# Spreading the weights' maxima by a product with an identity, and ten filler products per unit of the first batch

## The chip, the cores and the metric

The kernel runs on one core of one Trainium2 chip. The metric is the device time of one execution in microseconds (us); of several runs the median is given.

## The reference

Attention with queries pooled in pairs, followed by a feed-forward layer whose gate is h*cos(h):

```python
q_pool = q.reshape(B, H, S // 2, 2, D).mean(axis=3)          # 8, 8, 1152 -> 576, 64
scores = np.matmul(q_pool, k.transpose(0, 1, 3, 2)) / np.sqrt(D)
scores = scores - np.max(scores, axis=-1, keepdims=True)
attn = np.exp(scores)
attn = attn / (np.sum(attn, axis=-1, keepdims=True) + 1e-09)
x = np.matmul(attn, v)            # then (B*S/2, H*D) = (4608, 512)
h = x @ w_in                      # w_in: 512 x 2048
out = (h * np.cos(h)) @ w_out     # w_out: 2048 x 512
```

q, k and v are f32; the two weights are f64 and are read as pairs of 32-bit words.

## The kernel before

Attention runs over 32 pairs of heads (8 batches of 4 pairs). A pair is ten units: unit 0 takes the 64 rows of each head that fill no tile of 128, units 1 to 9 one block of 128 keys each. A unit has score products on TensorE into the PSUM tile st (one buffer of two banks, lines 851 and 871), exp on ScalarE, and, one unit later, the products with v into the PSUM tiles ava and avb, one for each head of the pair (`av`, lines 919 to 1000). In the first four pairs, which are the first batch (`p < NDIR`), the products with v take f32 operands, four a head and unit, and the trace shows two records for each; from the fifth pair on ScalarE and GpSimd (or VectorE) split exp into two f16 parts, and all products are f16. Beside the units run side jobs for later pairs: loads and transposes of q and k, a first pass of score products into the PSUM tile mx (line 646 and on) whose row maxima VectorE takes (mxs, line 656), and the maximum over all of v, which `all_max_begin` spreads over the partitions by way of DRAM (row, am).

The weights are prepared meanwhile. `weight_group` loads slices of 1 MB (wraw), takes each partition's maximum (wmx, line 437), puts the f64 words together as f32 (lines 444 to 450), and needs the maximum over all partitions for a power-of-two scale. To get it, it writes the column of maxima to DRAM (row, line 468), reads it back broadcast to all partitions (wam, line 470), gives the generator four idle steps (WBN), and reduces on VectorE (line 477) with some small operations behind (lines 479 to 490). ScalarE scales and casts, and GpSimd subtracts for the low part (lines 496 to 498). `weight_steps` (line 506) drives these groups: first w_in, two slices a group and two groups alive, then w_out, two slices a group and one group alive. The loop over the units steps it SRATE times a unit.

The feed-forward part (`ffn1`, line 1149, and `ffn2`, line 1205) works on chunks of 256 rows of x, interleaved with later pairs, from when the first batch's x is there, and ends the kernel alone.

What each engine runs in what order is written by `arrange`: it takes the recorded instructions with their dependences, lets a planner with a price for each instruction run them (the lowest place in the recorded order first among those that are ready), and fixes each engine's order by that. The DMAs all go through SP's queue, in order. The waits between engines come from the tiles that are written and read.

Of the kernel before, what the change touches and what calls it, by code (L numbers as in the profile page):

```python
# [19 lines left out]
P = 128  # L20
POW2_MASK = 0x7F800000
POW2_HIGH = 0x40000000
TINY = 1e-12
PMAX = 2.0**6
MDIV = 64.0
VLAG = 3
# [10 lines left out]
DFIRST = 0  # L37
WPOOL = 1
NDIR = 4
WLD = 2  # L40
WBN = 4
WGATE = 4
SRATE = 1.6
EWR = 2

_INS = ["q", "k", "v", "moe_w_in", "moe_w_out"]
# [8 lines left out]
SIZES = {"float32": 4, "uint32": 4, "int32": 4, "float16": 2}  # L55
SEM = 0.10
BOOST = {}


def boxes(ins):  # L60
# [63 lines left out]
    return wr[0][2] if wr else 1  # L124


def arrange(tc, nc, extra):

    rec = [i for i in nc.cur_bb.bb.instructions if "Boundary" not in type(i).__name__]
    nodes, last_pe = [], None  # L130
    for i in rec:
        rd, wr = boxes(i)
        eng = str(i.engine).split(".")[-1]
        if eng == "PE":
            key = wr[0][0].name
            if last_pe is not None and last_pe["key"] == key and len(last_pe["ins"]) < 12:
                nd = last_pe
            else:
                nd = last_pe = dict(eng=eng, ins=[], rd=[], wr=[], cost=0.0, lock=False, key=key)
                nd["tile"] = None  # L140
                nodes.append(nd)
            size = tuple(i.tile_size)
            c = max(n_out(wr) * 0.000421, 0.027)
            if rd[0][4] == 4:
                c = 0.3
            if size[0] == 64 and tuple(i.tile_position)[0] == 64:
                c = 0.0
            nd["cost"] += c
            nd["tile"] = size[0]
        else:  # L150
            nd = dict(eng=eng, ins=[], rd=[], wr=[], cost=0.0, lock=False)
            nodes.append(nd)
            if eng == "SP":
                nd["cost"] = 0.06
                nd["dma"], nd["lat"] = transfer(type(i).__name__, rd[0], wr[0])
            else:
# [10 lines left out]
    for k, nd in enumerate(nodes):  # L167
        deps = set()
        for w, lst in ((0, nd["rd"]), (1, nd["wr"])):
            for t, box, *_ in lst:  # L170
                name = t.name
                if name not in hist:
                    hist[name] = ([], [], set())
                    tag = getattr(t, "tag", None)
                    if tag:
                        base, pool = tag.rsplit("_", 2)[0:2]
                        nb = BUFS.get(base, POOL_BUFS.get(pool, 1))
                        ring = tags.setdefault(tag, [])
                        if pool != "fix" and len(ring) >= nb:
                            prev_tile[name] = ring[-nb]  # L180
                        if pool != "fix" and ring:
                            deps.add(first[ring[-1]])
                        ring.append(name)
                        first[name] = k
                reads, writes, users = hist[name]
                if name in prev_tile:
                    deps |= hist[prev_tile[name]][2]
                deps |= {j for j, bx in writes if hit(bx, box)}
                if str(t.space).endswith("PSUM"):
                    bank = (0, P, box[2] // 2048 * 2048, (box[3] - 1) // 2048 * 2048 + 2048)  # L190
                    deps |= {
                        j
                        for j, bx in reads
                        if hit(bx, bank)
                    }
                if w:
                    deps |= {j for j, bx in reads if hit(bx, box)}
        for w, lst in ((0, nd["rd"]), (1, nd["wr"])):
            for t, box, *_ in lst:
                reads, writes, users = hist[t.name]  # L200
                users.add(k)
                if w:
                    inside = lambda b: box[0] <= b[0] and b[1] <= box[1] and box[2] <= b[2] and b[3] <= box[3]
                    writes[:] = [x for x in writes if not inside(x[1])]
                    reads[:] = [x for x in reads if not inside(x[1])]
                    writes.append((k, box))
                else:
                    reads.append((k, box))
        deps.discard(k)
        nd["deps"] = deps  # L210
# [14 lines left out]
    for k, nd in enumerate(nodes):  # L225
        base = [t.tag.rsplit("_", 2)[0] for t, *_ in nd["rd"] + nd["wr"] if getattr(t, "tag", None)]
        off = 0
        for t in set(base):
            off = min(off, BOOST.get((nd["eng"], t), 0))
        nd["key"] = (k + off, k)  # L230

    engines = ("PE", "Activation", "DVE", "Pool", "SP")
# [79 lines left out]
def tile_attention_ffn(  # L312
# [91 lines left out]
    w1v = w_in.rearrange("(c p) f -> p c f", p=P)  # L404
    w2v = w_out.rearrange("(f p) e -> p f e", p=P)

    w1_ready = [False]
    gate = [None]
    hsc_live = [0]

    def weight_group(wi, i0, fts):
# [6 lines left out]
        for a, ft in enumerate(fts):  # L418
# [45 lines left out]
                    apply_absolute_value=True,  # L464
                )
            yield
        row = dram.tile([n, P], F32, tag="wrow", bufs=4, name="row")
        nc.sync.dma_start(row.rearrange("a p -> p a"), mx)
        am = sb2.tile([P, n, P], F32, tag="g", bufs=NG, name="wam")
        nc.sync.dma_start(  # L470
            am.rearrange("p a b -> p (a b)"),
            row.rearrange("a p -> (a p)").unsqueeze(0).broadcast_to([P, n * P]),
        )
        for _ in range(WBN):
            yield
        mw = sb2.tile([P, n], F32, tag="wmw", name="wmw")
        nc.vector.reduce_max(mw, am, axis=AX.X)
        if wide:
            nc.vector.tensor_scalar_max(mw, mw, 2.0**-15)
            mu = mw.bitcast(U32)  # L480
            ah = sb2.tile([P, n], U32, tag="wah", name="wah")
            nc.vector.tensor_scalar(ah, mu, POW2_HIGH, None, ALU.bitwise_and)
            nc.vector.tensor_scalar(
                mu, mu, 0x07FFFFFF, 3, ALU.bitwise_and, ALU.logical_shift_left
            )
            nc.vector.tensor_tensor(mu, mu, ah, ALU.bitwise_or)
        all_max_end(p2w[:, wi, i0 : i0 + n], mw)
        sc = sb2.tile([P, n], F32, tag="wsc", name="wsc")
        nc.vector.reciprocal(sc, p2w[:, wi, i0 : i0 + n])
        nc.vector.tensor_scalar_mul(sc, sc, 2.0**14)  # L490
        for a, ft in enumerate(fts):
            ds = slice((i0 + a) * width, (i0 + a + 1) * width)
# [13 lines left out]
    def weight_steps():  # L506
        stage = w2[1].rearrange("p f e -> p (f e)").bitcast(F32)
        live = []
        todo = [(wi, i) for wi in range(2) for i in range(0, NWP, 2)]
        done = 0  # L510
        while todo or live:
            if todo and len(live) < (2 if todo[0][0] == 0 else 1):
                wi, i = todo.pop(0)
                if wi == 0:
                    o = i % 4 * 1024
                    fts = [stage[:, o + a * 1024 : o + (a + 1) * 1024] for a in range(2)]
                else:
                    yt = sb1.tile([P, 2, 1024], F32, tag="y", name="wf")
                    fts = [yt[:, a] for a in range(2)]
                live.append(weight_group(wi, i, fts))  # L520
            for g in list(live):
                if next(g, 1) == 1:
                    live.remove(g)
                    done += 2
                    if done == NWP:
# [9 lines left out]
    extra = []  # L535

    def after(ins, prev):
        if prev is not None:
# [369 lines left out]
        return pps  # L908

    acc = [None, None]  # L910
    order = [None]
    xps = {}
    pairs_done = [0]
# [12 lines left out]
    def av(u, parts):  # L926
# [42 lines left out]
        j = i - 1  # L969
        pp = parts[0]  # L970
        if j == 0:
            acc[1] = psum.tile([P, 512], F32, tag="avb", name="avb")[
                :, 0 : QT * (D + 1)
            ].rearrange("p (t d) -> p t d", d=D + 1)
        if p < NDIR:
            for h in range(2):
                first = None
                for t in range(QT):
# [3 lines left out]
                    if start:  # L982
                        first = mm
                    elif first is not None:
                        after(mm, first)
        for part in range(2 if p >= NDIR else 0):
            for h in range(2):
                first = None
# [18 lines left out]
        for h in range(2):  # L1007
            n = QT + 1 - h
            rs = sb2.tile([P, QT + 1], F32, tag="rs", name="rs")
            nc.vector.tensor_scalar_add(rs[:, 0:n], acc[h][:, :, D], 1e-9 * PMAX)  # L1010
# [361 lines left out]
        if pump() is None:  # L1372
            break
    ev_flush()
    arrange(tc, nc, extra)


# [24 lines left out]
```

## Time and profile before

| what | us |
|---|---|
| median of three runs | 1702.73 |
| lowest and highest | 1696.87, 1713.77 |
| the profiled execution | 1703.86 |
| its span, first to last instruction | 1702.1 |
| TensorE busy in it | 1548.4 (91%) |
| VectorE busy | 1134.9 (67%) |
| ScalarE busy | 1216.5 (71%) |
| GpSimd busy | 887.0 (52%) |
| mean granted clock of TensorE | 0.953 |

In the profile PE is TensorE, PEld its weight loads, DVE VectorE, ACT ScalarE, POOL GpSimd, SP SyncE with the DMA queue. The granted clock is a share of 2.4 GHz: 1.00 is that level and 0.50 the level of 1.2 GHz; a value between is a mean over time at both. L851 is line 851 of the kernel. Times in a trace row are from the start of the span.

### The profile page before, as it was taken

The page shows a single profiled execution, that of the slowest core. Times are in us where ns is not written, and L with a number is a line of the kernel's source. Part 1 is how long each engine was busy: PE and PEld are TensorE (multiplying, and loading weights), DVE is VectorE, ACT ScalarE, POOL GpSimd, SP SyncE. Part 2 cuts the span into 40 slices and gives each one's busy share as a digit, 9 for nine tenths or more (in the row PEclk, how much of TensorE's full clock was granted, in tenths as well). Part 3 has the DMA queues.
Part 4 walks back from the last instruction along what each step waited for, and adds up shares of the span by engine and source line. Part 5 has one row for each costly group of instructions (what it writes and reads, how often), then busy time and mean ns, then how long its engine had stood idle before and what let it go on. Part 6 is the DMA issues. An engine that isn't in the chain of part 4 may idle for free.

```text
span 1702.1 us, 39816 instructions
## 1 busy us (share of the span) xinstructions
PE 1548.4 (91%) x16728; PEld 999.9 (59%) x16728; DVE 1134.9 (67%) x1618; ACT 1216.5 (71%) x1476; POOL 887.0 (52%) x763
## 2 busy tenths in 40 slices
PE   2688877899899989998999999899999999997998
PEld 0465655566566546654666566666666666665664
DVE  6667668777776667676877767577777768632342
ACT  2244447888798868876887787798798879884442
POOL 3133227647647565756665556466756575461222
PEclk9687779899999999999999999999999999998999
DMA  9968875233643554354624324434444442101000
GB/s 203 185 117 138 161 142 94 66 69 81 101 79 73 98 99 85 79 105 78 111 59 99 84 52 105 78 72 97 101 78 87 88 112 47 34 21 27 13 25 20
DMA packets 339893, 147.34 MB, mean 87 GB/s; under 512 B 246016, under 2 KB 322816, under 8 KB 339712
## 3 DMA queue, kind: packets, MB, share of 16 engines
q1 hardware_dynamic: 339712, 144.79, 42.9%
q8 instruction: 131, 2.15, 0.6%
q14 instruction: 50, 0.41, 0.1%
HBM read 77.59 MB, written 10.51 MB: 52 GB/s over the span
## 4 chain that ended last, share of the span: by engine, by line
PE 70%; DVE 9%; DMA 8%; ACT 5%; issue 3%; POOL 2%; SPq 1%; another core or an unknown queue 0%; POOLq 0%; ACTq 0%; DVEq 0%
PE f L1205 21%; PE f L1149 19%; PE st L851 12%; PE ava L919 7%; PE avb L919 5%; PE mx L646 4%; DVE mxs L656 2%; DMA qld<-in_q_dram 2%; ACT e L897 2%; DMA am<-row 1%; POOL pp L906 1%; DMA wam<-row 1%; PE mx L686 1%; PE st L871 1%; DMA wraw<-in_moe_w_out_dram 1%
## 5 line engine op out<-in xcount | busy, mean ns | idle before, releaser
L906 POOL TENSOR_TENSOR pp<-e,pp 128x512 f16<-128x512 f32 x374 | 448.3, 1220 | 312.1 <-ACT pp L900 131.5
L1149 PE MATMUL f<-xT,w 128*128 128x256 f16 x3456 | 415.2, 277 | 15.7 <-DVE y L1175 8.9
L897 ACT ACTIVATE e<-st,eb 128x1024 f32<-128x1024 f32 x280 | 311.4, 1112 | 134.4 <-PE st L851 102.8
L656 DVE TENSOR_REDUCE mxs<-mx 128x2 f32<-128x1024 f32 x252 | 307.6, 1221 | 149.6 <-PE mx L646 147.9
L1205 PE MATMUL f<-w,g 128*128 128x512 f16 x1728 | 395.5, 380 | 0.0
L1149 PEld LDWEIGHTS <-w 128*128 128x128 f16 x3456 | 332.0, 99 | 88.0 <-issue 40.2
L900 ACT CAST pp<-e 128x1024 f16<-128x1024 f32 x280 | 292.5, 1044 | 8.9 <-PE ava L919 0.9
L919 PEld LDWEIGHTS <-pp 128*128 128x128 f16 (+1 forms) x7392 | 242.8, 101 | 71.0 <-issue 21.0
L1205 PEld LDWEIGHTS <-g 128*128 128x128 f16 x1728 | 161.2, 98 | 194.4 <-issue 14.5
L1114 POOL TENSOR_TENSOR g<-hsc,g 128x512 f16<-128x512 f32 x144 | 192.2, 1361 | 152.7 <-ACT g L1113 143.2
L919 PE MATMUL ava<-vc,pp 128*128 128x64 f16 (+4 forms) x4784 | 259.0, 205 | 13.2 <-POOL pp L906 10.9
L851 PE MATMUL st<-q1T,k 128*128 128x512 f16 x576 | 228.8, 397 | 14.1 <-ACT e L897 10.0
L851 PE MATMUL st<-q2T,k 128*128 128x512 f16 x576 | 229.1, 398 | 0.0
L919 PE MATMUL avb<-vc,pp 128*128 128x65 f16 (+1 forms) x3312 | 215.4, 205 | 2.6 <-POOL pp L906 2.6
L1175 DVE SCALAR_TENSOR_TENSOR y<-f,r1a,y 128x512 f32<-128x512 f32 x144 | 106.8, 746 | 115.1 <-ACT y L1174 113.6
L851 PEld LDWEIGHTS <-k 128*128 128x128 f16 x1152 | 103.7, 102 | 107.1 <-issue 34.1
L1171 ACT ACTIVATE hsc<-f,r 128x512 f32<-128x512 f32 x144 | 98.3, 684 | 80.5 <-PE f L1149 80.0
L1104 DVE TENSOR_TENSOR hsc<-hsc,y 128x512 f32<-128x512 f32 x144 | 128.5, 942 | 40.3 <-ACT y L1098 39.9
L579 POOL TENSOR_TENSOR kst<-kld,kst 128x512 f16<-128x512 f32 x64 | 88.9, 1390 | 127.0 <-ACT kst L578 119.9
L646 PE MATMUL mx<-k,q1T 64*128 64x512 f16 x504 | 105.8, 415 | 54.0 <-DVE mxs L656 25.8
L902 DVE TENSOR_TENSOR pp<-e,pp 128x1024 f16<-128x1024 f32 x93 | 127.6, 1372 | 37.9 <-ACT pp L900 37.5
L646 PEld LDWEIGHTS <-q1T 64*128 64x128 f16 x512 | 26.8, 94 | 163.1 <-issue 125.9
(113 smaller groups left out, 1561.8 us busy)
## 6 DMA issues: line engine op xcount, KB each, us to landing
vld<-in_v_dram SPq DMA_DIRECT2D x32, 576.0 KB
qld<-in_q_dram SPq DMA_DIRECT2D x64, 256.0 KB
kld<-in_k_dram SPq DMA_DIRECT2D x32, 320.0 KB
kld<-in_k_dram SPq DMA_DIRECT2D x32, 256.0 KB
wraw<-in_moe_w_in_dram SPq DMA_DIRECT2D x8, 1024.0 KB
wraw<-in_moe_w_out_dram SPq DMA_DIRECT2D x8, 1024.0 KB
out_dram<-ob SPq DMA_DIRECT2D x32, 256.0 KB
k<-k SPq DMA_DIRECT2D x64, 80.0 KB
```

Of the source, the lines that this page charges most:

```text
L646: nc.tensor.matmul(m[:, h, :], q1T[n][HALF[h], 2 * t + h, :], k1[n % 3][HALF[h], c * RB : (c + 1) * RB, h, :], start=True, stop=True, skip ...
L656: nc.vector.reduce_max(mxs[n][:, 2 * t : 2 * t + 2, c], m, axis=AX.X)
L851: nc.tensor.matmul(s[:, h, :].rearrange("p (t c) -> p t c", c=P), w[:, j, h, :], x[:, h : 2 * QT : 2, :], start=part == 0, stop=part == 1, ...
L897: nc.scalar.activation(e, s, AF.Exp, scale=exp_scale, bias=eb)
L900: nc.scalar.copy(pp[:, 0], e)
L902: nc.vector.tensor_sub(pp[:, 1], e, pp[:, 0])
L906: nc.gpsimd.tensor_sub(pp[:, 1, c], e[:, c], pp[:, 0, c])
L919: mm = nc.tensor.matmul(out, w, x, start=start, stop=False, skip_group_check=True)
L1104: nc.vector.tensor_mul(hj, hj, y[:, j : j + 2])
L1114: nc.gpsimd.tensor_sub(gt[:, 1], hj, gt[:, 0])
L1149: mm = nc.tensor.matmul(ps[:, fi, :], w1[wt][:, hp, fs], ck.xT[hp][:, xi, cs], start=n == 0, stop=n == 3 * HP - 1, skip_group_check=True,)
L1205: nc.tensor.matmul(po, gt[:, gi, f % 2, ts_], w2[wt][:, f, :], start=f == 0 and (gi, wt) == (0, 0), stop=f == NF - 1 and (gi, wt) == (1, 0),)
```

## The change

The column of maxima is no longer sent through DRAM. An f32 product on TensorE takes it, broadcast along the free dimension, as the stationary operand and an identity as the moving one, into a PSUM tile of the feed-forward part's tag; VectorE reduces from there. The identity is made on GpSimd at the start. The four idle steps of a group go, two of its small operations on VectorE too, SRATE becomes 1.0, and w_out is prepared in groups of one slice, two alive.

In units 1 to 8 of each pair of the first batch, ten f16 products of the identity's bytes with 252 of its columns follow the products with v. They write to columns of avb's bank that nobody reads. The planner sees each as a node of its own at its place in the recorded order, prices an f32 product at 0.112 instead of 0.3, and puts writes to one bank in order.

```diff
-SRATE = 1.6
+SRATE = 1.0
+NFILL = 10
@@ arrange
-            key = wr[0][0].name
+            key = wr[0][0].name if i.name not in fill else i.name
             if rd[0][4] == 4:
-                c = 0.3
+                c = 0.112
                     bank = (0, P, box[2] // 2048 * 2048, (box[3] - 1) // 2048 * 2048 + 2048)
+                    deps |= {j for j, bx in reads if hit(bx, bank)}
+                    if w:
+                        deps |= {j for j, bx in writes if hit(bx, bank)}
@@ tile_attention_ffn
+    ident = sb2.tile([P, P], F32, tag="g", bufs=NG, name="ident")
+    nc.gpsimd.memset(ident, 0.0)
+    nc.gpsimd.affine_select(out=ident, in_=ident, compare_op=ALU.not_equal, fill=1.0,
...
@@ weight_group
-        row = dram.tile([n, P], F32, tag="wrow", bufs=4, name="row")
-        nc.sync.dma_start(row.rearrange("a p -> p a"), mx)
-        am = sb2.tile([P, n, P], F32, tag="g", bufs=NG, name="wam")
-        nc.sync.dma_start(
-            am.rearrange("p a b -> p (a b)"),
-            row.rearrange("a p -> (a p)").unsqueeze(0).broadcast_to([P, n * P]),
-        )
-        for _ in range(WBN):
-            yield
+        am = psum.tile([P, n, P], F32, tag="f", bufs=2, name="wam")
+        for a in range(n):
+            nc.tensor.matmul(
+                am[:, a, :],
+                mx[:, a : a + 1].broadcast_to([P, P]),
+                ident,
...
         mw = sb2.tile([P, n], F32, tag="wmw", name="wmw")
         nc.vector.reduce_max(mw, am, axis=AX.X)
+        pw = p2w[:, wi, i0 : i0 + n]
         if wide:
-            nc.vector.tensor_scalar_max(mw, mw, 2.0**-15)
+            nc.vector.tensor_scalar_max(mw, mw, W64_MIN)
...
-                mu, mu, 0x07FFFFFF, 3, ALU.bitwise_and, ALU.logical_shift_left
-            )
-            nc.vector.tensor_tensor(mu, mu, ah, ALU.bitwise_or)
-        all_max_end(p2w[:, wi, i0 : i0 + n], mw)
+                mu, mu, 0x07F00000, 3, ALU.bitwise_and, ALU.logical_shift_left
+            )
+            nc.vector.tensor_tensor(pw.bitcast(U32), mu, ah, ALU.bitwise_or)
@@ weight_steps
-        todo = [(wi, i) for wi in range(2) for i in range(0, NWP, 2)]
+        todo = [(0, i) for i in range(0, NWP, 2)] + [(1, i) for i in range(NWP)]
-            if todo and len(live) < (2 if todo[0][0] == 0 else 1):
+            if todo and len(live) < 2:
...
-                    fts = [yt[:, a] for a in range(2)]
+                    fts = [yt[:, i % 2]]
@@ av, behind the f32 products with v of one unit
+            i16 = ident.bitcast(F16)
+            for _ in range(NFILL if i < NU - 1 else 0):
+                fm = nc.tensor.matmul(
+                    rest[0],
+                    i16[:, 0:P],
+                    i16[:, 0 : 512 - QT * (D + 1)],
+                    start=False,
+                    stop=False,
+                    skip_group_check=True,
+                )
+                after(fm, mm)
+                fill.add(fm.ins.name)
+                fills.append(fm)
...
+            while h and fills:
+                after(ra, fills.pop())
```

`rest[0]` is the part of avb's bank behind the 260 columns of the products with v.

## Rows read from the trace of the kernel before

**Rows 1.** Part 2 of the page: TensorE's busy tenths and granted clock, forty slices.

```profile
PE   2688877899899989998999999899999999997998
...
PEclk9687779899999999999999999999999999998999
```

**Rows 2.** Windows: us; busy (x instructions) PE, PEld, DVE, ACT, POOL; PEclk, DMA, GB/s.

```profile
36.80:97.75 60.95, 44.47 (x260) 29.30 (x259) 40.43 (x52) 20.44 (x22) 16.15 (x13) 0.72 0.80 165
97.75:147.50 49.75, 40.51 (x274) 29.96 (x273) 36.39 (x60) 22.06 (x24) 11.20 (x6) 0.76 0.81 138
147.50:202.30 54.80, 42.77 (x294) 30.31 (x294) 37.23 (x67) 24.80 (x30) 19.02 (x15) 0.78 0.76 138
202.30:251.75 49.45, 38.53 (x285) 27.38 (x284) 35.62 (x61) 20.58 (x24) 10.73 (x9) 0.83 0.82 159
251.75:274.70 22.95, 18.65 (x265) 12.52 (x265) 20.11 (x27) 18.67 (x23) 19.15 (x15) 0.99 0.77 99
274.70:345.00 70.30, 58.07 (x673) 41.02 (x673) 52.76 (x73) 56.23 (x66) 41.61 (x36) 0.88 0.30 74
```

**Rows 3.** Waits of VectorE, 36 to 275 us: total us, times, longest.

```profile
DVE wmw L477 <- DMA wam<-row: 11.4, 3, 6.3
DVE amx L397 <- DMA am<-row: 10.4, 2, 6.5
DVE wmx L437 <- DMA wraw<-in_moe_w_out_dram: 7.1, 1, 7.1
...
DVE wmx L437 <- DMA wraw<-in_moe_w_in_dram: 3.0, 1, 3.0
```

**Rows 4.** Waits of TensorE, the same stretch and columns.

```profile
PE mx L646 <- DVE mxs L656: 21.4, 7, 5.4
```

**Rows 5.** The chain that ended last, in order of time: start, us, what.

```profile
92.59 8.69 DMA wam<-row
...
119.96 9.72 DMA row<-wmx
...
181.43 1.90 PE ava L919 x8
183.32 1.71 PE avb L919 x8
185.03 1.71 PE st L851 x4
...
196.30 0.89 PE ava L919 x8
197.20 0.86 PE st L851 x4
```

**Rows 6.** Windows of 5 us, columns as in rows 2.

```profile
175.00:180.00 5.00, 0.00 (x0) 0.00 (x0) 0.65 (x1) 0.00 (x0) 0.00 (x0) 0.86 1.25 168
...
190.00:195.00 5.00, 5.00 (x20) 3.17 (x20) 0.12 (x1) 2.51 (x4) 4.80 (x5) 0.50 0.43 52
195.00:200.00 5.00, 5.00 (x34) 3.76 (x35) 4.93 (x6) 1.93 (x4) 1.13 (x1) 0.93 0.75 219
```

**Rows 7.** Waits of SP's queue, 0 to 300 us.

```profile
SPq L470 <- DMA row<-wmx: 12.5, 3, 5.5
```

**Rows 8.** Groups by line on VectorE, 36.8 to 251.8 us: one small operation.

```profile
L401 DVE TENSOR_SCALAR wmw<-wmw 128x2 f32<-128x2 f32 x7 | 1.2, 169 | 0.2
```

**Rows 9.** Timeline of GpSimd at the start; in brackets the idle time before.

```profile
0.73 1.06 POOL L358 MEMSET qs<- 128x1152 f16 x1 [0.29 <-POOLq L1383]
...
9.60 1.40 POOL L585 TENSOR_TENSOR qld<-qld 128x576 f32<-128x576 f32 x1 [4.16 <-DMA qld<-in_q_dram]
```

**Rows 10.** Timeline of TensorE in the feed-forward part.

```profile
313.16 5.40 PE L1149 MATMUL f<-xT,w 128*128 128x256 f16 x48
```

**Rows 11.** Windows of the instructions on slices of weights (wraw): DVE busy, PEclk, DMA, GB/s.

```profile
251.75:274.70 22.95, 5.54 (x5) 0.99 0.77 99
274.70:345.00 70.30, 3.67 (x3) 0.88 0.30 74
```

More of the change, by code (lines that the diff above doesn't have):

```diff
@@ L23 @@
 TINY = 1e-12
+W64_MIN = 0.05859375
 PMAX = 2.0**6
@@ L57 @@
 BOOST = {}
+FILL_LATE = 0
+COLD = 0
 def boxes(ins):
@@ L124, in n_out, with arrange @@
     return wr[0][2] if wr else 1
-def arrange(tc, nc, extra):
+def arrange(tc, nc, extra, fill):
     rec = [i for i in nc.cur_bb.bb.instructions if "Boundary" not in type(i).__name__]
@@ L143, in arrange @@
             c = max(n_out(wr) * 0.000421, 0.027)
+            if COLD and i.name in fill:
+                c = 0.112
             if rd[0][4] == 4:
-                c = 0.3
+                c = 0.112
             if size[0] == 64 and tuple(i.tile_position)[0] == 64:
@@ L190, in arrange @@
                     bank = (0, P, box[2] // 2048 * 2048, (box[3] - 1) // 2048 * 2048 + 2048)
[L191 to L195, printed above, removed]
+                    deps |= {j for j, bx in reads if hit(bx, bank)}
+                    if w:
+                        deps |= {j for j, bx in writes if hit(bx, bank)}
                 if w:
@@ L229, in arrange @@
             off = min(off, BOOST.get((nd["eng"], t), 0))
+        if nd["ins"][0].name in fill:
+            off = FILL_LATE
         nd["key"] = (k + off, k)
@@ L405, in tile_attention_ffn @@
     w2v = w_out.rearrange("(f p) e -> p f e", p=P)
+    ident = sb2.tile([P, P], F32, tag="g", bufs=NG, name="ident")
+    nc.gpsimd.memset(ident, 0.0)
+    nc.gpsimd.affine_select(
+        out=ident,
+        in_=ident,
+        compare_op=ALU.not_equal,
+        fill=1.0,
+        base=0,
+        pattern=[[-1, P]],
+        channel_multiplier=1,
+    )
     w1_ready = [False]
@@ L466, in weight_group @@
             yield
-        row = dram.tile([n, P], F32, tag="wrow", bufs=4, name="row")
-        nc.sync.dma_start(row.rearrange("a p -> p a"), mx)
-        am = sb2.tile([P, n, P], F32, tag="g", bufs=NG, name="wam")
-        nc.sync.dma_start(
-            am.rearrange("p a b -> p (a b)"),
-            row.rearrange("a p -> (a p)").unsqueeze(0).broadcast_to([P, n * P]),
-        )
-        for _ in range(WBN):
-            yield
+        am = psum.tile([P, n, P], F32, tag="f", bufs=2, name="wam")
[4 more added lines that the diff above has]
+                ident,
+                start=True,
+                stop=True,
+                skip_group_check=True,
+            )
         mw = sb2.tile([P, n], F32, tag="wmw", name="wmw")
         nc.vector.reduce_max(mw, am, axis=AX.X)
+        pw = p2w[:, wi, i0 : i0 + n]
         if wide:
-            nc.vector.tensor_scalar_max(mw, mw, 2.0**-15)
+            nc.vector.tensor_scalar_max(mw, mw, W64_MIN)
             mu = mw.bitcast(U32)
@@ L483, in weight_group @@
             nc.vector.tensor_scalar(
-                mu, mu, 0x07FFFFFF, 3, ALU.bitwise_and, ALU.logical_shift_left
+                mu, mu, 0x07F00000, 3, ALU.bitwise_and, ALU.logical_shift_left
             )
-            nc.vector.tensor_tensor(mu, mu, ah, ALU.bitwise_or)
-        all_max_end(p2w[:, wi, i0 : i0 + n], mw)
+            nc.vector.tensor_tensor(pw.bitcast(U32), mu, ah, ALU.bitwise_or)
+        else:
+            all_max_end(pw, mw)
         sc = sb2.tile([P, n], F32, tag="wsc", name="wsc")
-        nc.vector.reciprocal(sc, p2w[:, wi, i0 : i0 + n])
+        nc.vector.reciprocal(sc, pw)
         nc.vector.tensor_scalar_mul(sc, sc, 2.0**14)
@@ L508, in weight_steps @@
         live = []
-        todo = [(wi, i) for wi in range(2) for i in range(0, NWP, 2)]
+        todo = [(0, i) for i in range(0, NWP, 2)] + [(1, i) for i in range(NWP)]
         done = 0
+        yt = None
         while todo or live:
-            if todo and len(live) < (2 if todo[0][0] == 0 else 1):
+            if todo and len(live) < 2:
                 wi, i = todo.pop(0)
@@ L517, in weight_steps @@
                 else:
-                    yt = sb1.tile([P, 2, 1024], F32, tag="y", name="wf")
-                    fts = [yt[:, a] for a in range(2)]
+                    if yt is None:
+                        yt = sb1.tile([P, 2, 1024], F32, tag="y", name="wf")
+                    fts = [yt[:, i % 2]]
                 live.append(weight_group(wi, i, fts))
@@ L523, in weight_steps @@
                     live.remove(g)
-                    done += 2
-                    if done == NWP:
+                    done += 1
+                    if done == NWP // 2:
                         w1_ready[0] = True
@@ L535, in tile_attention_ffn @@
     extra = []
+    fill = set()
     def after(ins, prev):
@@ L910, in tile_attention_ffn @@
     acc = [None, None]
+    rest = [None]
+    fills = []
     order = [None]
@@ L971, in av @@
         if j == 0:
-            acc[1] = psum.tile([P, 512], F32, tag="avb", name="avb")[
-                :, 0 : QT * (D + 1)
-            ].rearrange("p (t d) -> p t d", d=D + 1)
+            bank = psum.tile([P, 512], F32, tag="avb", name="avb")
+            acc[1] = bank[:, 0 : QT * (D + 1)].rearrange("p (t d) -> p t d", d=D + 1)
+            rest[0] = bank[:, QT * (D + 1) :]
         if p < NDIR:
@@ L985, in av @@
                         after(mm, first)
+            i16 = ident.bitcast(F16)
[6 more added lines that the diff above has]
+                    stop=False,
+                    skip_group_check=True,
+                )
+                after(fm, mm)
+                fill.add(fm.ins.name)
+                fills.append(fm)
         for part in range(2 if p >= NDIR else 0):
@@ L1009, in av @@
             rs = sb2.tile([P, QT + 1], F32, tag="rs", name="rs")
-            nc.vector.tensor_scalar_add(rs[:, 0:n], acc[h][:, :, D], 1e-9 * PMAX)
+            ra = nc.vector.tensor_scalar_add(rs[:, 0:n], acc[h][:, :, D], 1e-9 * PMAX)
+            while h and fills:
+                after(ra, fills.pop())
             nc.vector.reciprocal(rs[:, 0:n], rs[:, 0:n])
@@ L1374, in tile_attention_ffn @@
     ev_flush()
-    arrange(tc, nc, extra)
+    arrange(tc, nc, extra, fill)
 def kernel(**inputs):
```

## The prediction

> **What bounds the kernel now.** I read the page's forty slices first [rows 1]. From the ninth slice on TensorE is busy nine tenths or more almost everywhere at a granted clock of nine tenths or more: there the kernel is bound by TensorE, and a microsecond saved before that stretch is a microsecond off the end. The first eight slices are different: two to eight tenths busy, and a clock of six to eight tenths in six of them. The change is made there, so I cut that part at the pairs of heads [rows 2]: four pairs of the first batch from 36.8 to 251.75 us (215 us), then the start of the feed-forward part up to 345 us (93 us). In the first, TensorE is busy 44.47+40.51+42.77+38.53 = 166.3 us and idle 48.7; VectorE is busy 149.7. Neither is full, so I looked for what they wait for.
>
> Two things show. **Waits for DMA on VectorE** [rows 3]: 11.4 us for the spread maxima of the weights (wam), 10.4 us for those of v (am), 7.1 and 3.0 us for a slice of weights. VectorE runs in order and the row maxima of the scores (mxs) queue behind; TensorE then waits for those, 21.4 us in one line's products alone [rows 4]. The chain of waits runs through the same transfers: 8.69 us for one wam, 9.72 us for the row it is read from [rows 5]. **The clock** [rows 6]: TensorE is idle at 175 to 180 us; it is busy for all of 190 to 195 us at 0.50, which is the 1.2 GHz level, and comes back only after 195 us. The same eight records of the first batch's f32 products take 1.90 and 1.71 us in that stretch, 0.89 us behind it; the four score products 1.71 and 0.86 us [rows 5]. By the mean clocks of rows 2 the low level holds 2x(0.28x60.95 + 0.24x49.75 + 0.22x54.8 + 0.17x49.45) = 99 us of the 215, 46%.
>
> The Trainium skill, "TensorE: Matmul & The Clock Gate" (What's actually happening), says the gate opens by how busy the engine has lately been. Rows 6 agree only in part: an engine busy 5.00 of 5.00 us stayed at the low level, so what the profile calls busy is not what releases it, and by the page's letter alone fillers would add nothing here that the engine had not already; that outcome, at 1729 us, is the third rival below.
>
> **The change, part by part.**
> *Maxima by TensorE.* Removed: 8 pairs of small transfers and their places in SP's queue, which stood 12.5 us behind the row transfers [rows 7], with the waits of rows 3 for wam, 11.4 us. Added: 16 f32 products with an identity. The trace has no 128-column f32 product; the nearest is the 65-column one, 0.89/8 = 0.11 us a record at the high level [rows 5] and two records a product. Between the same and twice that: 16x2x(0.11 to 0.22) = 3.5 to 7 us; I take 5, as 128 columns at both levels lie nearer the upper end. Small operations on VectorE: 9 a group in 8 groups before, 7 in 12 groups after, 12 more of 0.17 us [rows 8] = 2 us. The identity is two small operations on GpSimd, which stood idle 4.16 us before its first work on q [rows 9]; by its 1.06 us memset of 1152 columns two operations on 128 fit. If that cover fails it costs the start 1 to 2 us.
> A new dependence: TensorE, in order, now stands at each product until VectorE has the slice's maximum, and that waits for the slice. The two late slices are 10.1 us [rows 3]; VectorE, and so mxs, stood for them before too, so I charge nothing, and 10 us as the other end.
>
> *Fillers.* Eight units of each pair, four pairs, ten each: 320 products of 252 f16 columns. Nearest row: 48 products of 256 columns in 5.40 us, 0.1125 us each [rows 10]; at the low level twice that. So 36 us at the high level, 53 us at the present mix (36x1.46). What they buy is the low level's excess: 99 us x the busy share 166.3/215 = 76 us of work at half speed, 38 us excess. Cured by all (38) or by nothing (0)? The fillers follow a unit's f32 products directly and stand ahead of f16 score products, so an uninterrupted f16 stretch of some 2 us at the high level (1.125 + 0.86) takes the place of one of 0.86. I take three quarters, 28.5, since the stalls on v's maxima and on late slices stay. With a quarter of the low level left the fillers cost 40.
>
> The skill's table (same page, Why this matters for your kernels) wants no idle gaps between bursts; it speaks against the fillers as far as they queue in order behind a stalled product and cannot fill that gap. The trace agrees: the low level of rows 6 begins behind an idle stretch. By the rule alone the cure is the share of the waits that goes with wam, 11.4 of 31.9 us: 14 us instead of 28.5, TensorE at 198, and by the working below 207 for the four pairs and 1690 at the end.
>
> *Order of the weights.* Counting the generator's steps, 80 at 1.6 a unit end at unit 49 before, 40 at 1.0 at unit 39 after. So weight work that today lies behind 251.75 us, 5.54+3.67 = 9.2 us of VectorE [rows 11], moves into the four pairs, with its ScalarE and GpSimd parts, engines that are busy 20 to 25 us of a 50 us pair at most [rows 2]. The planner's price of an f32 product falls from 0.3 to 0.112; with the added products' dependences this reorders, and I price it at nothing, bounded by the scatter of the runs, some 8 us either way.
>
> **The sum.** Four pairs. TensorE: 166.3 - 28.5 + 40 + 5 = 183 us. VectorE: 149.7 + 9.2 + 2 = 161, and with the waits that stay (10.4 + 10.1) 181. So fillers make the two about equal, and neither work nor waits allow less than 183. Today the longer of the two is VectorE with its waits, 149.7 + 31.9 = 181.6, and the stretch takes 215, 1.18 times that. If that ratio stays, it will be 183x1.18 = 217, no gain; if coupling were perfect, 183, a gain of 32. The ratio comes from an alternation: at the low level VectorE starves, behind it VectorE is full and TensorE waits [rows 4]. A steady clock takes away part of it, and fillers that stand ahead of a wait lie in idle time. I take the middle, 200: a gain of 15.
> Start of the feed-forward part: idle 4.3 + 12.2 = 16.5 us, and the low level holds 2x0.12x70.3 = 17 us [rows 2]. 9.2 us of VectorE's weight work leave. Gain 0 to 16; I take 6.
> The profiled execution is 1703.86 us (span 1702.1), 1.1 us over the median of 1702.73. 1703.9 - 15 - 6 = **1683 us**.
>
> **Rivals.**
> *The clock holds and VectorE has little left to wait* (0.17): four pairs in 183, start 16 less: 1703.9 - 32 - 16 = 1656 us. For it: 31.9 us of waits and 99 us of low level in one stretch. Against: VectorE would have to run without a gap.
> *Fillers eat what they buy* (0.30): 36 to 40 us of new work against 28.5 to 38 us of excess; the wam waits go, but the late slices and v's maxima take their place, or TensorE stands at its new products. Four pairs 215, start 0 to 6 less: 1700 us.
> *The fillers do not release the clock* (0.13): TensorE 166.3 + 53 + 5 = 224 us. Of the 48.7 us idle, 11.4 go with wam and I let the fillers cover 18; 19 stay. 243 us, 28 more than 215; less 0 to 6: some 1729 us. It decides if the granted clock of the four pairs stays below about 0.85. For it: rows 6, a full engine at 0.50. Against: from the ninth slice on, where all products are f16, the clock is high [rows 1].
> That the waits for wam go is not in doubt, as the transfers are gone.
>
> **How the numbers follow.** The forecast has 0.40, its own range 1668 to 1696 us (half of either gain more or less). 1% is 17 us and about what a measurement of this kernel can tell, as its three runs span 1696.87 to 1713.77. Below 1686 lie the first rival and most of the forecast: 0.17 + 0.34 = 0.51. Within 1%: the second rival and the rest, 0.36. Slower by over 1%: the third, 0.13. The range must leave out no more than 0.2: 1652 takes in the first rival, 1712 the second with the scatter; outside lie the third and small tails.
>
> **What would show it.** Right: granted clock of the four pairs at 0.9 or more, their length near 200 us, filler records near 0.11 us, no wait of VectorE for a spread maximum of weights, feed-forward starting some 15 us earlier, its first 70 us with less idle time. Wrong: long stretches at 0.50 behind stalls on am or on slices of weights; TensorE standing at the new products; VectorE saturated while TensorE waits; or a later part of the span that changes by more than the 8 us I allowed for the order.

## The result and the profile after

The changed kernel takes 1690.27 us, median of nine runs (1683.38 to 1698.10); the kernel before, measured with it, 1702.73 (1695.50 to 1713.77). The ratio is 0.9915 with a 95% interval of 0.9888 to 0.9941: faster by 0.6 to 1.1%, where 1683 us and 1.2% were forecast. The profiled execution spans 1688.5 us against 1702.1.

Part 2 of the page after, TensorE's busy tenths and granted clock in forty slices (compare [rows 1]):

```profile
PE   2899678999799989998999999999999999997998
...
PEclk9899898999899999999999999999999999998999
```

The clock of the second to eighth slice, six to nine tenths before, is eight or nine now. By pairs, cut as in [rows 2] at the first score product of each pair's unit 0 (columns as there), the first six pairs:

```profile
36.11:90.76 54.65, 44.61 (x334) 32.93 (x333) 39.62 (x51) 20.57 (x23) 16.12 (x13) 0.88 0.71 177
90.76:135.34 44.58, 43.46 (x397) 34.28 (x395) 38.28 (x59) 23.28 (x25) 15.97 (x10) 1.00 0.80 169
135.34:182.34 47.00, 43.58 (x388) 34.19 (x385) 34.91 (x63) 24.02 (x28) 15.83 (x9) 0.96 0.59 130
182.34:238.46 56.12, 43.16 (x372) 34.00 (x371) 44.03 (x77) 24.63 (x28) 15.51 (x12) 0.88 0.59 139
238.46:292.99 54.53, 41.07 (x465) 27.04 (x464) 44.18 (x64) 37.19 (x43) 29.88 (x25) 0.84 0.42 88
292.99:344.42 51.43, 49.25 (x583) 32.92 (x580) 38.98 (x52) 48.21 (x59) 33.63 (x29) 1.00 0.25 55
```

The first three pairs take 146.2 us instead of 165.5 (from 36.8 to 202.3 before); the fourth takes 56.1 instead of 49.5, and the fifth 54.5 where it took 38.9 (its start at 251.75 to the next at 290.63). So the fourth and fifth give back 22 us, more than the 19 that the first three win; the sixth then takes 51.4 instead of 59.6. (Part of this is feed-forward work that is done earlier, counted below.) Windows of 5 us show where TensorE stands (same columns):

```profile
190.00:195.00 5.00, 0.80 (x5) 0.38 (x4) 4.83 (x9) 1.48 (x3) 3.70 (x2) 0.79 0.89 229
195.00:200.00 5.00, 0.98 (x6) 0.51 (x6) 4.86 (x10) 3.39 (x5) 2.20 (x2) 0.50 0.60 127
...
245.00:250.00 5.00, 1.78 (x6) 0.44 (x4) 4.93 (x4) 3.18 (x4) 3.77 (x2) 0.75 0.18 53
250.00:255.00 5.00, 1.22 (x4) 0.31 (x4) 4.72 (x14) 2.49 (x5) 3.54 (x3) 0.50 0.39 118
```

VectorE is full, TensorE stands, and the clock falls to the low level behind it. The waits of VectorE from 36 to 275 us, as [rows 3]:

```profile
DVE mxs L680 <- PE mx L670: 23.4, 15, 7.4
DVE mxs L720 <- PE mx L710: 14.2, 2, 8.5
DVE amx L403 <- DMA am<-row: 3.4, 2, 2.8
```

No wait for a spread maximum of the weights is left, none for a late slice, and 3.4 us for v's maxima instead of 10.4. What is left is waiting for TensorE, up to 8.5 us at a time: all its waits for TensorE come to 41.4 us, where the kernel before had 31.1 in this stretch. And TensorE's own (compare [rows 4]):

```profile
PE mx L670 <- DVE mxs L680: 18.5, 10, 3.8
...
PE wam L487 <- DVE wmx L455: 1.0, 2, 0.7
```

TensorE hardly stands at its new products. A unit's fillers in the timeline of TensorE (start, us):

```profile
207.63 1.24 PE L1014 MATMUL avb<-ident 128*128 128x252 f16 x10
208.70 0.38 PE L875 MATMUL st<-q1T,k 128*128 128x512 f16 x1
```

Ten take 1.07 us from the first's start to the next product, 0.107 us each at the high level.

In long windows, the four pairs, the part from there to the start of the seventh pair, and the rest. The kernel before, behind its four pairs:

```profile
251.75:350.18 98.43, 80.25 (x997) 55.89 (x997) 77.14 (x104) 79.59 (x96) 64.17 (x53) 0.91 0.42 81
350.18:1702.10 1351.92, 1294.64 (x14598) 825.13 (x14597) 887.91 (x1248) 1041.53 (x1274) 754.80 (x652) 0.98 0.36 74
```

and the changed one:

```profile
36.11:238.46 202.35, 174.80 (x1484) 135.40 (x1483) 156.84 (x247) 92.51 (x104) 63.43 (x43) 0.92 0.67 154
238.46:344.42 105.96, 90.32 (x1041) 59.96 (x1040) 83.16 (x115) 85.40 (x101) 63.51 (x54) 0.92 0.34 72
344.42:1688.50 1344.08, 1281.73 (x14529) 818.57 (x14527) 883.31 (x1243) 1032.09 (x1263) 751.92 (x652) 0.98 0.37 75
```

At the start of the seventh pair the changed kernel is 5.8 us ahead (344.42 against 350.18). It has also done more of the feed-forward part by then: windows of those products' line from 0 to that point, first the kernel before, then the two lines of the changed one,

```profile
0.00:350.18 350.18, 29.81 (x240) 24.19 (x240) 0.83 0.72 136
```

```profile
0.00:344.42 344.42, 34.88 (x288) 27.36 (x288) 0.93 0.60 133
0.00:344.42 344.42, 11.03 (x48) 4.40 (x48) 0.93 0.60 133
```

48 products of 256 columns more, and 48 of 512 where there were none: 5.4 us and twice that at the pace of [rows 10], 16 us. So it is 22 us of work ahead. The rest of the span is only 7.8 us shorter, though it has those 16 us less to do: 8 us are lost there, 5 of them as idle time of TensorE (57.3 us before, 62.4 after, length less busy time).

### The profile page after: what moved, and what is told of

The parts are those of the page before. It is cut to its first block, busy times and chain, and to the rows that moved or that the text cites. A ratio compares the mean times of both kernels' runs of the same rounds, so it can differ in the third digit from the quotient of the medians.

```text
span 1688.5 us, 40499 instructions
## 1 busy us (share of the span) xinstructions
PE 1554.1 (92%) x17080; PEld 1015.9 (60%) x17080; DVE 1142.9 (68%) x1630; ACT 1217.3 (72%) x1476; POOL 890.2 (53%) x765
## 5 line engine op out<-in xcount | busy, mean ns | idle before, releaser
L945 PE MATMUL ava<-vc,pp 128*128 128x64 f16 (+4 forms) x4784 | 250.0, 203 | 19.4 <-POOL pp L930 17.9
L875 PE MATMUL st<-q1T,k 128*128 128x512 f16 x576 | 222.3, 386 | 18.5 <-ACT e L921 12.1
L875 PE MATMUL st<-q2T,k 128*128 128x512 f16 x576 | 222.2, 386 | 0.0
L945 PE MATMUL avb<-vc,pp 128*128 128x65 f16 (+1 forms) x3312 | 205.4, 201 | 3.2 <-POOL pp L930 3.0
L1145 DVE TENSOR_TENSOR hsc<-hsc,y 128x512 f32<-128x512 f32 x144 | 131.1, 959 | 36.7 <-ACT y L1139 36.1
```

Of the source, the lines that this page charges most:

```text
L875: nc.tensor.matmul(s[:, h, :].rearrange("p (t c) -> p t c", c=P), w[:, j, h, :], x[:, h : 2 * QT : 2, :], start=part == 0, stop=part == 1, ...
L945: mm = nc.tensor.matmul(out, w, x, start=start, stop=False, skip_group_check=True)
L1145: nc.vector.tensor_mul(hj, hj, y[:, j : j + 2])
```

## The experiments

Each ratio is to the kernel before, run beside it on the same chip. It is worked out from the single runs and isn't the quotient of the two medians, from which it differs by up to 0.0024 (experiment 5: 0.9921). The kernel before itself had medians of 1702.7 to 1720.6 us on the five occasions, so ratios of different occasions are compared only where they are far apart. Kernels 1 to 4, then 5 to 8, then 9 to 11 were measured on one occasion each, the changed kernel and 12 each on its own.

**1. Without the fillers.**

```diff
-NFILL = 10
+NFILL = 0
```

> The changed kernel without its 320 fillers; the product with the identity, the order of the weights and the prices stay. Theory A (the fillers pay through the clock: they save the low level's excess of 38 us and cost 34 to 40, but lie largely in idle time): granted clock of the four pairs falls back below 0.9, four pairs at 205 to 215 us, end at 1695 to 1705 us, ratio to before 0.995 to 1.0. Rival B (the gain is the missing waits for the spread maxima, the fillers only eat what they buy): four pairs at 195 to 203 us, end within 3 us of the changed kernel or below it, ratio 0.985 to 0.992.

Measured: 1712.74 us against 1718.0, ratio 0.9963 (0.9941 to 0.9986). Long windows, four pairs and the part behind:

```profile
36.88:248.16 211.28, 160.83 (x1165) 118.18 (x1163) 156.47 (x245) 92.45 (x103) 63.70 (x46) 0.78 0.62 148
248.16:355.24 107.08, 93.39 (x1040) 61.54 (x1039) 83.42 (x117) 84.74 (x101) 59.11 (x50) 0.88 0.35 69
```

The clock is back at 0.78 and the four pairs at 211 us: as theory A said. The 320 products cost TensorE 14 us of busy time here, net of what the clock gives back, and the stretch is 9 us shorter with them. Product, order and price without the fillers keep a gain of 0.1 to 0.6%.

What the fillers do to the clock shows in stretches at the low level in which TensorE is not idle at all. The longest one in the four pairs, cut at whole microseconds, in the kernel before, here, in experiment 12 (which has no fillers either) and in the changed kernel:

```profile
69.00:89.00 20.00, 20.00 (x75) 12.89 (x74) 10.04 (x22) 7.50 (x8) 3.74 (x3) 0.50 1.09 185
58.00:85.00 27.00, 27.00 (x124) 21.33 (x123) 10.02 (x18) 8.72 (x8) 4.26 (x3) 0.50 0.42 111
163.00:185.00 22.00, 22.00 (x122) 18.50 (x121) 10.07 (x13) 3.96 (x4) 1.40 (x1) 0.50 0.41 96
57.00:67.00 10.00, 10.00 (x54) 7.90 (x52) 1.84 (x3) 2.37 (x3) 2.38 (x2) 0.52 0.74 212
```

Without fillers a TensorE that is busy all the time stays at 1.2 GHz for 20 to 27 us. With ten f16 fillers a unit no such stretch in any run is longer than 10. How the fillers end it is not shown.

**2. The fillers alone**, on the kernel before: the identity, `rest`, the loop of fillers and what the planner needs for them; everything else as before.

> The kernel before with the 320 fillers alone (and the planner's bank rule and nodes that they need); the maxima still go through DRAM, and the order of the weights and the price 0.3 stay. Theory A: the granted clock of the four pairs rises to 0.9 or more except behind the stalls on wam, four pairs at 203 to 210 us, ratio to before 0.993 to 0.998. Rival B: the clock rises, but the time of the fillers is lost again, and the waits for wam stay: ratio 1.0 to 1.006.

Measured: 1747.84 us, ratio 1.0168 (1.0141 to 1.0195). Both expected too little: the four pairs take 255 us.

```profile
36.26:291.64 255.38, 188.16 (x1417) 136.71 (x1416) 164.09 (x251) 91.07 (x103) 65.17 (x46) 0.87 0.72 130
```

The clock did rise, from 0.77 to 0.87. VectorE's waits from 36 to 350 us:

```profile
DVE mxs L668 <- PE mx L658: 34.7, 17, 9.2
DVE wmw L488 <- DMA wam<-row: 18.9, 5, 7.3
```

The waits for wam, which the other half of the change removes, became longer than in [rows 3]: 18.9 against 11.4 us, and it stays 11.4 when that window, too, is taken to 350 us.

**3. Five fillers a unit.**

```diff
-NFILL = 10
+NFILL = 5
```

> The changed kernel with five fillers a unit instead of ten, 160 in all, some 17 us of TensorE less. If the clock holds with five as with ten (0.93 or more in the four pairs), theory A expects 3 to 8 us below the changed kernel, ratio 0.987 to 0.990. If five do not hold it (clock below 0.88), it lies between the kernel without fillers and the changed one.

Measured: ratio 0.9896 (0.9863 to 0.9929).

```profile
37.43:242.90 205.47, 167.68 (x1324) 124.25 (x1323) 158.86 (x246) 92.05 (x103) 61.02 (x44) 0.85 0.64 151
```

The four pairs take 205.5 us at a mean clock of 0.85. So five hold the clock less well than ten, against the first branch: 0.78, 0.85 and 0.92 with none, five and ten, and so it is wherever five and ten were both run: 0.87 against 0.94 at 0.8 steps a unit (experiments 8 and 7), 0.87 against 0.91 at the price 0.3 (11 and 5). They also cost less, and the end can't be told from that of the changed kernel, where the second branch put it behind that.

**4. f32 fillers.**

```diff
-NFILL = 10
+NFILL = 4
                 fm = nc.tensor.matmul(
-                    rest[0],
-                    i16[:, 0:P],
-                    i16[:, 0 : 512 - QT * (D + 1)],
+                    rest[0][:, 0:P],
+                    ident,
+                    ident,
```

> The changed kernel with four f32 products of 128 columns a unit in place of the ten f16 ones: about the same time of TensorE, so the engine is as busy as with the fillers. If being busy is what releases the clock, the granted clock of the four pairs is that of the changed kernel (above 0.9). If the kind of product matters, it is near that of the kernel before (0.72 to 0.83), and the four pairs take 215 to 240 us.

One profiled run: 1727.8 us, beside a median of 1718.0 for the kernel before.

```profile
36.53:265.13 228.60, 188.58 (x1421) 145.06 (x1419) 155.97 (x245) 92.13 (x104) 63.62 (x44) 0.83 0.56 136
```

The clock of the four pairs is 0.83: above the 0.78 of no fillers, below the 0.92 of f16 fillers. TensorE is busy for more microseconds than with those (188.6 against 174.8), but for less of its stretch (82% against 86%). And with the ten f16 fillers unchanged the clock runs from 0.84 to 0.94 in the experiments that order the work otherwise (2, 5, 6, 7, 9 and 10). So one run at 0.83 can't tell the kind of product from the order: neither theory is decided, and what in a product counts is left open.

**5. The old price of an f32 product.**

```diff
-                c = 0.112
+                c = 0.3
```

> The changed kernel with the planner's old price of 0.3 for an f32 product; fillers, product and order of the weights stay. Background: the fillers alone made the kernel before slower, four pairs 255 us against 215, so one of the other parts is needed for them. Theory P (it is the price: at 0.3 the planner holds a unit of the first batch for longer than it is and puts more of the weights' work between two units): four pairs at 225 to 250 us, ratio 1.005 to 1.02. Theory D (it is the way through DRAM, whose waits of 18.9 us hold VectorE behind a fuller TensorE): within 6 us of the changed kernel, ratio 0.988 to 0.996.

Measured: 1690.97 us, ratio 0.9897 (0.9851 to 0.9943). The price is not what the fillers need. Where the work stands does change: the four pairs take 210 us, 8 more, with VectorE busy 175.8 of them, and the part behind takes 96 us, 10 less.

**6. Fillers and the new price on the kernel before.** Experiment 2 with the price of 0.112.

> The kernel before with the fillers and the new price 0.112, the maxima still through DRAM. Theory P: four pairs at 205 to 220 us, ratio 0.992 to 1.003. Theory D: still slower, four pairs at 240 to 255 us, ratio 1.01 to 1.02.

Measured: 1724.12 us, ratio 1.0104 (1.0068 to 1.0140). Theory D has the end right and theory P the length of the four pairs:

```profile
37.28:252.73 215.45, 179.40 (x1414) 135.10 (x1413) 152.37 (x231) 87.33 (x98) 56.19 (x42) 0.86 0.75 144
252.73:362.88 110.15, 86.33 (x1009) 60.81 (x1007) 75.33 (x111) 80.64 (x96) 66.03 (x53) 0.86 0.41 84
```

The four pairs are as long as in the kernel before, and the part behind them is 12 us longer. The price thus accounts for most of what experiment 2 lost in the four pairs (255 us there). The last maximum of a slice is taken at 285.8 us, against 252.9 in the kernel before. A late end of the weights doesn't explain the loss, though: experiment 2 has it at 243.4 us and loses more, experiment 9 at 268.4 and gains. Nor do the waits for wam, which are 8.1 us here and were 11.4. Why the fillers cost 1% here is not shown.

**7. Slower weights.**

```diff
-SRATE = 1.0
+SRATE = 0.8
```

> The changed kernel with the weights stepped 0.8 times a unit instead of 1.0, so that they end in the recorded order at unit 49 and no longer at 39. Theory: VectorE, full from 185 to 215 and from 238 to 262 us in the changed kernel, is what holds TensorE there; spread over more units the weights leave it room. Four pairs at 192 to 200 us, but more work behind them; end between 4 us below and 4 us above the changed kernel. Rival (the feed-forward part waits for the end of the weights in the recorded order): slower by 5 to 15 us, ratio 0.995 to 1.0.

Measured: 1704.98 us, ratio 0.9988 (0.9961 to 1.0015): the whole gain is lost, within the rival's range.

```profile
36.92:225.08 188.16, 168.34 (x1435) 129.91 (x1433) 141.72 (x220) 85.78 (x97) 53.67 (x41) 0.94 0.69 153
225.08:350.05 124.97, 92.08 (x1036) 65.55 (x1034) 100.93 (x138) 83.91 (x100) 69.67 (x54) 0.84 0.39 82
```

The four pairs win 14 us against the changed kernel and the part behind loses 19; VectorE's work only moved. The length of the four pairs is thus no measure of the end.

**8. Five fillers and slower weights.** Both edits.

> Five fillers a unit and the weights stepped 0.8 times a unit. If both hold what they promise alone, 2 to 8 us below the changed kernel, ratio 0.986 to 0.990; if the slower weights cost, as the run with ten fillers at 0.8 then shows too, ratio 0.993 to 1.0.

Measured: ratio 0.9993 (0.9973 to 1.0014), the same as with ten fillers at this rate.

**9. The old order of the weights.**

```diff
-SRATE = 1.0
+SRATE = 1.6
+        for _ in range(WBN):
+            yield
-        todo = [(0, i) for i in range(0, NWP, 2)] + [(1, i) for i in range(NWP)]
+        todo = [(wi, i) for wi in range(2) for i in range(0, NWP, 2)]
-            if todo and len(live) < 2:
+            if todo and len(live) < (2 if todo[0][0] == 0 else 1):
-                    if yt is None:
-                        yt = sb1.tile([P, 2, 1024], F32, tag="y", name="wf")
-                    fts = [yt[:, i % 2]]
+                    yt = sb1.tile([P, 2, 1024], F32, tag="y", name="wf")
+                    fts = [yt[:, a] for a in range(2)]
```

> The changed kernel with the old order of the weights: 1.6 steps a unit, the four idle steps kept, w_out in groups of two slices with one alive; product, fillers and price 0.112 stay. So it differs from the run of fillers and price on the kernel before (ratio 1.010) by the product alone, and from the changed kernel (0.9915) by the order alone. If the way through DRAM is what spoils the fillers there: 0.990 to 0.996, four pairs below 205 us. If it is the late end of the weights: 1.000 to 1.010, with the feed-forward part starting behind 275 us, as with 0.8 steps a unit (283 us, 0.999).

Measured: 1697.99 us against 1720.55, ratio 0.9849 (0.9812 to 0.9886), better than either branch; the four pairs are below 205 us, as the first had it.

```profile
36.35:234.64 198.29, 175.24 (x1443) 134.34 (x1441) 154.84 (x217) 86.96 (x98) 58.48 (x42) 0.91 0.66 152
234.64:333.83 99.19, 79.89 (x986) 57.17 (x984) 78.67 (x107) 77.96 (x92) 60.57 (x50) 0.91 0.43 92
```

Against experiment 6 it differs by the product alone (and the two small operations that go with it), and the step is from 1.010 to 0.985. The new order of the weights isn't needed for the gain; whether it costs something was not compared on one occasion.

**10. Faster weights.**

```diff
-SRATE = 1.0
+SRATE = 1.25
```

> The changed kernel with 1.25 weight steps a unit, the end of the weights in the recorded order at unit 31 instead of 39. At 0.8 (unit 49) the four pairs took 188 us, 14 less than at 1.0, and the part behind them lost 26. If that trade is monotone, the four pairs grow to 205 to 220 us and the part behind shrinks by as much or less; the end within 8 us of the changed kernel, ratio 0.988 to 0.997. If an early end is pure gain: below 0.987.

Measured: 1720.06 us, ratio 0.9985 (0.9959 to 1.0010). The four pairs grow to 236 us, beyond what was expected, and the gain is gone as at 0.8. (The 26 us in the expectation are against the kernel before; against the changed kernel the part behind lost 19.) An early end of the weights is no gain by itself.

**11. Five fillers and the old price.** Experiments 3 and 5 together.

> Five fillers a unit and the old price 0.3, each of which alone came out at 0.990. If the gains add: 0.986 to 0.989. If both only stir the order: 0.988 to 0.996, no different from the changed kernel.

Measured: 1684.09 us against 1720.55, ratio 0.9775 (0.9734 to 0.9816). Against the changed kernel's 0.9915 each edit alone stood 0.2% lower, which is within the intervals; together they stand 1.4% lower, if the occasions may be compared.

```profile
37.12:234.25 197.13, 168.40 (x1293) 123.27 (x1292) 171.18 (x267) 93.34 (x104) 71.24 (x46) 0.87 0.69 162
234.25:331.70 97.45, 89.39 (x1071) 62.26 (x1069) 69.15 (x95) 83.64 (x100) 57.10 (x51) 0.98 0.33 70
```

It is the fastest kernel here by its own time and by its ratio. VectorE is busy 171.2 of 197.1 us in the four pairs, and TensorE 89.4 of 97.5 us behind them at a clock of 0.98: here both parts are short at once. Why this pairing lands so well, where each edit alone moved little, is not shown.

**12. The product alone.** Experiment 9 without fillers.

```diff
-NFILL = 10
+NFILL = 0
```

> The product with the identity alone: as the run with the old order of the weights (0.985), but without fillers; the price 0.112 stays. It closes the square of way of the maxima and fillers under one order of the weights: the fillers with the way through DRAM cost 1.0% (1.010). If the two parts simply add, the product alone is near 0.975. If the fillers pay only once the stalls on wam are gone, the product alone lies above the run with both, 0.988 to 0.998, with the granted clock of the four pairs at 0.75 to 0.85 and the low level behind the stalls that stay.

Measured: 1719.62 us against 1719.36, ratio 0.9987 (0.9959 to 1.0015).

```profile
37.26:250.61 213.35, 171.55 (x1147) 126.53 (x1145) 147.54 (x211) 87.12 (x98) 58.24 (x42) 0.73 0.60 140
```

So the two parts don't add to 0.975; the ratio is just above the second branch's range, and the clock just below its own. What became of the waits shows in VectorE's, 36 to 275 us, the kernel before first:

```profile
DVE mxs L656 <- PE mx L646: 23.8, 11, 6.1
```

```profile
DVE mxs L681 <- PE mx L671: 24.7, 10, 8.9
DVE mxs L721 <- PE mx L711: 18.2, 4, 8.8
DVE mxs L699 <- PE mx L689: 15.9, 3, 10.1
```

In sum its waits for DMA fall from 31.9 to 1.5 us, and its waits for TensorE rise from 31.1 to 60.5: the waits for transfers give way to waits for a TensorE at a mean clock of 0.73.

Under the old order of the weights, ratio to the kernel before, and the four pairs with TensorE's busy time, its idle time and the clock:

| maxima | fillers | ratio | four pairs us | busy | idle | clock |
|---|---|---|---|---|---|---|
| through DRAM | none (before) | 1 | 215.0 | 166.3 | 48.7 | 0.77 |
| product | none (12) | 0.9987 | 213.4 | 171.6 | 41.8 | 0.73 |
| through DRAM | ten (6) | 1.0104 | 215.5 | 179.4 | 36.1 | 0.86 |
| product | ten (9) | 0.9849 | 198.3 | 175.2 | 23.1 | 0.91 |

(The three with an edit have the price 0.112, the kernel before 0.3; the new price alone, without fillers or product, was not run. Experiments 2 and 6 show what it changes with the fillers alone, 1.017 and 1.010.) If the two parts added, and the price did nothing, both together would stand at 1.009. They stand at 0.985. For the parts to add, the price alone would have to make the kernel before 2.4% slower; the largest step of the price seen here is 1.2% (experiments 3 and 11). So it is likely, though not shown, that the parts gain more together than apart. What stands at one price: the fillers take 1.4% off the kernel with the product (0.5% in the new order of the weights, experiment 1), and the product 2.5% off the kernel with the fillers. With the product in place the fillers add 3.6 us to TensorE's busy time and take 18.7 from its idle time. On the way through DRAM they add 13.1 and take 12.6, and the part behind grows. With the product alone the clock is 0.73, and TensorE is busy 5 us longer.

## Why the prediction held, and where it was off

*What bounds the kernel, and that TensorE's late start passes to the end*: right in kind. At the seventh pair 22 us of work were gained, where the sum had 15 + 6 = 21; 13.6 arrived at the end of the span. That the four pairs came out at 202 where 200 was forecast is partly luck: the terms below were off both ways.

*TensorE's term, 183 us*: measured 174.8, so the excess that went was larger or the price smaller than I took. The fillers' price was right, 0.107 us against 0.1125. The mean clock rose to 0.92: the low level holds 2x0.08x202 = 32 of 202 us instead of 99 of 215, two thirds cured where I took three quarters.

*VectorE's term, 161 us and 181 with its waits*: measured 156.8, and 160 with the one DMA wait left. The step that said the waits for v's maxima and for late slices would stay was wrong: 20.5 us were to stay and 3.4 did. In their place the waits for TensorE, which the term left out, rose from 31.1 to 41.4 us.

*The ratio of 1.09 for coupling*: this is the term that was mis-sized, and its error was covered by the two before. The four pairs took 202.35 us, 1.16 times TensorE's 174.8, nearly the old 1.18. The alternation did not go away: it moved to the fourth and fifth pair, where VectorE is full, in part with slices of weights and the small operations on their maxima, and TensorE stands (the windows at 190 and 245 us).

*Start of the feed-forward part, a gain of 6*: by the clock 7.5 us were lost there (105.96 against 98.43), but with 16 us more work done in it; on equal work a gain of 8. The working mixed length and work.

*The order, priced at nothing within 8 us*: 8 us were lost behind the seventh pair, about the difference between the forecast and the result. That the order lost them is argued, not shown. Experiments 7 and 10 show how much such a term can be: the rate of the weights' steps alone, a quarter up or a fifth down, takes away the whole gain.

*The two parts*: the sum treated the missing waits and the clock as terms that add. By the table above they most likely don't: in experiment 12 the waits for DMA that went came back as waits for TensorE. The forecast was near because the change makes both; for either alone this working would have promised a gain, and neither experiment 6 nor 12 has one.

*The variant with a cure of 14 us*: its 207 us don't follow from the sum's own ratio, by which a TensorE at 198 gives 198 to 234 us, 216 in the middle, and an end near 1699. That its 1690 is what was measured is chance; TensorE's term was 174.8.

*The signs*: of those named for right, the clock (0.92), the filler's time, the missing waits and the earlier feed-forward part (238.5 against 251.75 us) are there. The first 70 us of that part have as much idle time as before (13.9 against 14.2). One sign named for wrong is there too, VectorE full while TensorE waits.

*The rivals.* That VectorE would have little left to wait for, with four pairs in 183 us, is refuted: they took 202, and VectorE waited 41.4 us for TensorE. That the clock would not be released is refuted: 0.92 with fillers, 0.78 without in experiment 1. That fillers eat what they buy is what happens without the product (experiment 6). Its named cause, late slices and TensorE standing at new products, can't be it there, as that kernel has no such products; in the changed kernel those cost 1.0 us. The Trainium skill's page "TensorE: Matmul & The Clock Gate" (What's actually happening) lets busy time open the gate; the kernel before has TensorE busy for 20.00 of 20.00 us at 0.50, so here the trace speaks against reading it as the profile's busy time. The Trainium skill's wish for no gaps (same page, Why this matters for your kernels) agrees with the windows at 190 to 200 us, where an engine busy 0.98 of 5.00 us is granted 0.50.

## What to carry to other kernels

Remove a stall and fill the engine's gaps as one change, and measure the four corners: here, with the planner's price changed beside each, the product alone was worth nothing, the fillers alone less, and both together 1.5%. Give the price a run of its own, which is missing here. Count work done as well as time passed when two schedules are compared at one point; a stretch that became shorter may only have passed its work on (188 us of four pairs at no gain, 197 at the largest gain). Where a planner orders everything, try its rates and prices beside the change: they moved the end by as much as the change did.

## What the runs showed of the hardware

The same kernel had medians of 1702.7, 1704.4, 1718.0, 1719.4 and 1720.6 us on the five occasions, a spread of 1.1%, more than the effect in question. The record gives one chip number for 1704.4 and 1719.4, so the spread isn't shown to be one between chips. Only ratios to runs made beside could show the effect.

An f32 weight load of 128 columns takes about twice an f16 one: in the changed kernel the medians (the middle of the three numbers, ns) are

```profile
L1014 PEld LDWEIGHTS <-ident x320: 95/98/253, 61.5 to 236.1; 128*128 128x128 f16 x160
...
L487 PEld LDWEIGHTS wam<-ident,wmx x32: 185/190/338, 50.4 to 244.8; 128*128 128x128 f32 x32
```

190 against 98 ns. And a TensorE that the profile shows busy without a gap can be granted 0.50 for 20 to 27 us (the kernel before, experiments 1 and 12), and for 10 at most in the runs with ten f16 fillers a unit.
